# A two-layer decode step on one core: scores of a head first, then the weighted sum of the head ahead

## The chip, the cores and the metric

The kernel runs on one core of one Trainium2 chip. The metric is the device time of one execution in microseconds. Before the change it is 2555.6 us, the median of three runs (2555.37 to 2556.39). A core has five engines that run side by side and synchronise by semaphores: TensorE (matrix products, PE in the profile), VectorE (DVE), ScalarE (ACT), GpSimd (POOL) and SyncE (SP). Sixteen DMA engines move data from HBM into the on-chip memory; here all transfers are issued by SyncE, in one fixed order.

## The reference

Two layers of the same weights. Each layer normalises x (2 batch entries, 576 columns), attends over a cached K and V, adds, then runs a mixer with a gated two-matrix network, and adds again:

```
q = (LN(x) @ wq) as 32 heads of 128
p = softmax(q . K / sqrt(128))          # K: 2 x 32 x 16384 x 128, bf16
x = x + (p @ V) @ wo                    # V like K
y = LN(x); h = gelu(LN(y) @ w1); hs = shift(h) @ w2
x = x + (y + hs) + gelu(LN(y + hs) @ w3) @ w4     # w3: 576 x 4608, w4: 4608 x 576
```

With one token the shifts along the sequence leave only zeros, so hs is the product of zeros with w2. The cache is 64 tiles (2 batch entries x 32 heads) of K and 64 of V, each 16384 x 128 in bf16, 4.19 MB. Both layers read the same cache.

## The kernel before

The memory `mem` holds six slots of one cache tile each, and ahead of them a small area for three buffers of transposed K (`kt`), which also takes weights between the attentions. A tile lies as 128 partitions of 128 rows of 128, so one transfer has 128 pieces of 32 KB. `plan_all` writes out every transfer with its place, in one list. `Store.pump` issues the next entry as soon as the program has given back all the cells under it (`Store.release`); SyncE then waits at that entry for the instructions that read those cells last, and everything behind it waits too. At the end of layer 0 three K tiles and two V tiles stay in memory (`held`), so layer 1 starts with head 63, then 61, 62, 0, 1 and so on (`order`). In this stretch slot 0 takes the weights wo, w3, w4 and layer 1's wq, one into the place of another: w3's first block into the place of the first group of wo, w4's groups into the places of w3's blocks.

A head (`attention`, the loop over s) has 128 blocks of 128 cache rows. Half are scored on TensorE: a chunk of eight blocks is transposed (L1161), copied by ScalarE into `kt` (L1177) and multiplied with q as a column (L1187), with the scores two chunks behind the transposes (`LEAD`). The other half is scored on VectorE in four pieces, a product with q spread over all partitions (L1218) and a sum (L1222), in `dots`. `softmax_max` takes the maximum of both parts (L1228, L1230, L1232) and over the partitions on GpSimd (L1235); `softmax_exp` takes the exponentials on ScalarE (L1243 to L1249); `pv` multiplies V in four pieces of 32 blocks (L1275). `q_broadcast` prepares q of the next head: a column (L1112), a diagonal (L1118), a product with ones (L1122), a copy (L1125). While head s is scored, the PV of head s - 1 is done: chunks 0 to 3 of head s, then each of the chunks 4 to 7 followed by one piece of PV. `landed` (relayed by GpSimd, L187) tells TensorE and VectorE that a tile has come.

The loop runs over heads 1 to 63 as 21 turns of three heads, on TensorE, ScalarE and VectorE (`Graph.loop`, `_loop`). The loop's first instruction is set at slot 0 of an instruction block on each of the three engines. At the end of a turn each engine lowers the semaphores it has used by what one turn adds.

After the loop `last_head` finishes head 63: softmax, `shares` (sums of exponentials, L927), `normed`, `dealt` (the heads' outputs put in the order that wo needs, L950 to L961), PV and five groups of wo (`heads_projection`, L903). `two_norms` then does both layer norms ahead of w3 from one set of sums, `cols_projection` multiplies w3 (L830, L840), `gelu` follows, and `groups_projection` multiplies w4 in eight groups (L903). In layer 0, `ahead` and `lay` use free moments of this stretch to transpose and copy 16 chunks of layer 1's first K tile (14 chunks to be laid, two held over), so that layer 1 can begin with `early_scores` (L1203).

Of the kernel before, what the change touches and what calls it, by code (L numbers as in the profile page):

```python
# [32 lines left out]
class Graph:  # L33
# [72 lines left out]
    def loop(self, first, turns, step):  # L106

        for e, a in first.items():
            n = len(self.ops[e]) - a
            assert n % turns == 0  # L110
            self.loops.append((e, a, n // turns, turns, step))
# [33 lines left out]
    def emit(self):  # L145
# [8 lines left out]
        for e, first, n, turns, _ in self.loops:  # L154
# [38 lines left out]
        def runner(e):  # L193
# [3 lines left out]
            def run(eng):  # L197
                seen, taken = {}, {}
                i = 0
                while i < len(ops):  # L200
                    if i in loops:
                        n, turns, step = loops[i]
                        self._loop(eng, e, i, n, turns, step, taken, seen, sems, wait, needs, emit_op)
                        i += n * turns
                        continue
# [12 lines left out]
    def _loop(self, eng, e, first, n, turns, step, taken, seen, sems, wait, needs, emit_op):  # L218
# [29 lines left out]
        for k, v in per.items():  # L248
            most = max(need.get(k, 0) for need in rel)
            assert most >= v > 0, (e, k, v, most)  # L250
        assert all(v > 0 for need in rel for v in need.values())
        me = eng.engine
        with self.nc.Fori(0, (turns - 1) * step + 1, step, engines=OrderedEngineSet([me]), head_slot={me: 0}) as turn:
# [79 lines left out]
class KB:  # L333
# [14 lines left out]
    PK = ["prod", "gT", "hf", "every"]  # L348
    GROUPS = (6, 6, 6, 6, 6, 3, 2, 1)

# [158 lines left out]
    def plan_all(self):  # L509
# [22 lines left out]
        self.plan_cols("w3", 0, self.w3, [full(0, mt, a), full(1, mt, a + w3r), full(2, mt, a + 2 * w3r),  # L532
                                          full(4, mt, a + 3 * w3r), (3, 0, mt // 2, 0), (3, mt // 2, mt, a)])
# [212 lines left out]
    def two_norms(self, l):  # L746
# [6 lines left out]
        self.scale_of()  # L753
        self.stt(s[:, 4, :], s[:, 2, :], -LN_EPS, hm[:, 1, :], ALU.mult, ALU.add, ["s2", "hm"], ["s4"])
        self.tt(s[:, 5, :], self.mv[:, 0, :], hm[:, 0, :], ALU.mult, ["mv", "hm"], ["s5"])
        self.tt(s[:, 5, :], self.mv[:, 2, :], s[:, 5, :], ALU.subtract, ["mv", "s5"], ["s5"])
        self.stt(s[:, 5, :], s[:, 5, :], 2.0, s[:, 3, :], ALU.mult, ALU.mult, ["s5", "s3"], ["s5"])
        self.tt(s[:, 4, :], s[:, 4, :], s[:, 5, :], ALU.add, ["s4", "s5"], ["s4"])
        self.recip(s[:, 6, :], s[:, 4, :], ["s4"], ["s6"])
# [3 lines left out]
        self.centred(self.x, "x")  # L763
        self.tt(self.kb(self.y0), self.kb(self.xc), self.over_k(s[:, 3, :]), ALU.mult, ["prod", "s3"], ["prod"])
        self.tt(self.kb(self.y), self.kb(self.y0), self.hsc[:, :, :], ALU.add, ["prod", "hsc"], ["prod"])
        self.tt(self.xn[:, :, :], self.kb(self.y), self.over_k(s[:, 7, :]), ALU.mult, ["prod", "s7"], ["xn"])

    def between_norms(self):
# [3 lines left out]
        self.tt(self.x1[:, 0:n, :], y0[:, 0:n, :], self.hs[:, 0:n, :], ALU.add, ["prod", "hs"], ["x1"])  # L772
        self.tt(self.x1[TL:, n, :], y0[TL:, n, :], self.hs[TL:, n, :], ALU.add, ["prod", "hs"], ["x1"])
        self.dv(lambda e: e.tensor_copy(out=self.xb[:, 0:n, :], in_=y0[:, 0:n, :]), reads=["prod"], writes=["xb"])
        self.dv(lambda e: e.tensor_copy(out=self.xb[TL:, n, :], in_=y0[TL:, n, :]), reads=["prod"], writes=["xb"])
# [225 lines left out]
    def attention(self, l):  # L1001
# [5 lines left out]
        def step(s, c, more):  # L1007
            h, u = c // n, o[s]
            if more:
                self.transposes(l, s, u, c)  # L1010
                pend.append((s, u, c, self.chunk))
                self.chunk += 1
                self.evacuate(pend[-1][3])
            while len(pend) > LEAD:
                self.scores(*pend.pop(0))
        if l == 0:
# [6 lines left out]
            for c in range(2 * n):  # L1023
                step(0, c, True)
                if c % n in (0, 2):
                    self.dots(l, 0, o[0], c // n, c % n // 2)
                if c == 2 * n - 2:
                    self.q_broadcast(1)
        else:
# [3 lines left out]
            for h, b, col in sorted(self.early):  # L1033
                self.early_scores(l, o[0], h * self.BP + b, col)
                if (h, b) == (0, self.CH):
                    self.q_broadcast(1)
            self.store.claim("kt", 0, self.AUX)
            for x in pend:
                self.evacuate(x[3])
            w = self.NB - 2 * self.PB  # L1040
            self.dv(lambda e: e.tensor_copy(out=self.s_dve[0][:, 0:w], in_=self.sps[2][:, 2 * self.PB:self.NB]),
                    reads=[("sps", 2)], writes=[("s_dve", 0)], to="vector")
        first = self.g.mark()
        for s in range(1, U):
            u, before = o[s], o[s - 1]
            self.landed("k", u, True)
            for c in range(2 * n):
                step(s, c, True)
                if c % n in (0, 2):
                    self.dots(l, s, u, c // n, c % n // 2)  # L1050
                if c == 2 * n - 2:
                    self.q_broadcast(s + 1)
# [312 lines left out]
```

## Time and profile before

| | |
|---|---|
| median of three runs | 2555.6 us |
| the profiled execution | 2555.16 us |
| its span, first to last instruction | 2553.4 us |
| mean granted TensorE clock | 0.572 |
| busy: PE, DVE, ACT, POOL | 64%, 74%, 48%, 6% |
| read from HBM | 1094.21 MB, 429 GB/s over the span |

How to read it: the page gives each engine's busy time, the span in 40 slices, the DMA queues, the chain of work that ended last, and groups of instructions. In a row by stretch the columns are: from and to, length, busy time and count of PE, PEld (weight loads), DVE, ACT and POOL, then the granted TensorE clock, the share of time in which the DMA engines were busy, and the rate in GB/s. In a timeline row they are: start, duration, engine, line, operation, output and inputs, shape, count, and in brackets the idle time ahead of it with what ended it. In a row of a group they are: busy time and mean ns of one, then idle time with its releaser. In a row of DMA issues the last column is the median time from issue to landing.

### The profile page before, as it was taken

Reading aid. Unit: us, or ns where it says so; the run is one execution under the profiler, and the core shown is the slowest. Engines: PE = TensorE matmul, PEld = TensorE weight load, DVE = VectorE, ACT = ScalarE, POOL = GpSimd, SP = SyncE. Lnnn points to the kernel's source line nnn. Section 1 sums busy time; section 2 is a strip of 40 time slices with the busy share of each in tenths; the row PEclk is TensorE's granted clock in tenths of the full one; section 3 lists DMA queues with packets and bytes.
Section 4 is the critical chain, followed back from the end, with each engine's and each line's share of the span. In section 5 each row is a group of like instructions: output and inputs, shape, how many; then the busy total and the mean of one; then the engine's idle time right before and its main releaser. Section 6 shows DMA issues by size and latency. Waiting matters only on the chain.

```text
span 2553.4 us, 75093 instructions
## 1 busy us (share of the span) xinstructions
PE 1629.1 (64%) x34456; PEld 1592.5 (62%) x34456; DVE 1889.3 (74%) x1924; ACT 1215.6 (48%) x1831; POOL 160.5 (6%) x151
## 2 busy tenths in 40 slices
PE   3766666656666665666687756666665666666566
PEld 3766566656656665666677756656665666666565
DVE  4877777777777777777649877777777777777774
ACT  2544444544444454444456544444454444445442
POOL 0000000000000000000000000000000000000000
PEclk8555655555555555555555565555555555555555
DMA  9999999999999999999999999999999999999999
GB/s 410 429 433 431 432 432 431 432 431 433 431 432 432 432 433 430 434 430 432 424 398 428 431 432 432 431 432 431 433 431 433 431 431 433 432 432 431 432 432 383
DMA packets 44761, 1094.82 MB, mean 429 GB/s; under 512 B 4906, under 2 KB 6318, under 8 KB 9390
## 3 DMA queue, kind: packets, MB, share of 16 engines
q1 hardware_dynamic: 44718, 1094.23, 99.9%
q8 instruction: 29, 0.48, 0.1%
q14 instruction: 14, 0.11, 0.0%
HBM read 1094.21 MB, written 0.00 MB: 429 GB/s over the span
## 4 chain that ended last, share of the span: by engine, by line
DMA 63%; DVE 21%; issue 9%; PE 5%; DVEq 0%; SPq 0%; ACT 0%; POOLq 0%; ACTq 0%
DMA mem<-in_A_k_cache_dram 61%; DVE prod L1218 10%; DVE s_dve L1222 9%; DMA mem<-in_B_w_dram 2%; PE tps L1161 2%; PE mps L1275 2%; PE sps L1122 1%; DMA mem<-in_A_wq_dram 0%; PE sps L1187 0%; DVE diag L1118 0%; PE sps L903 0%; DVE mx L1232 0%; DVE q_col L1112 0%; DVE o_acc L1256 0%; DVE mx L1230 0%
## 5 line engine op out<-in xcount | busy, mean ns | idle before, releaser
L1177 ACT ACTIVATE mem<-tps 128x1024 bf16<-128x1024 bf16 x1018 | 1030.1, 1024 | 848.5 <-PE tps L1161 826.8
L1222 DVE TENSOR_REDUCE s_dve<-prod 128x16 f32<-128x2048 bf16 x508 | 1161.2, 2286 | 17.4
L1161 PE MATMUL tps<-ident,mem 128*128 128x128 bf16 x8256 | 1011.0, 301 | 152.9 <-POOLq L187 148.1
L1218 DVE TENSOR_TENSOR prod<-mem,qb 128x2048 bf16<-128x2048 bf16 x508 | 621.3, 1223 | 534.0 <-POOLq L187 512.2
L1275 PE MATMUL mps<-p,mem 128*128 128x1 bf16 x16384 | 515.5, 166 | 605.7 <-ACT p L1249 605.7
L1275 PEld LDWEIGHTS mps<-p,mem 128*128 128x128 bf16 x16384 | 487.8, 105 | 616.5 <-ACT p L1249 616.4
L1161 PEld LDWEIGHTS tps<-ident,mem 128*128 128x128 bf16 x8256 | 770.0, 136 | 162.5 <-POOLq L187 157.4
L1187 PEld LDWEIGHTS sps<-q_col,mem 128*128 128x128 bf16 x8144 | 410.5, 113 | 5.0 <-ACT mem L1177 4.8
L1187 PE MATMUL sps<-q_col,mem 128*128 128x1 bf16 x8144 | 398.2, 170 | 4.3 <-ACT mem L1177 4.1
L1235 POOL PARTITION_ALL_REDUCE mx<-mx x128 | 158.6, 1239 | 2339.4 <-DVE mx L1232 2339.4
L1243 ACT ACTIVATE mx<-mx 128x1 f32<-128x1 f32 x128 | 25.9, 203 | 338.8 <-POOL mx L1235 338.8
L1122 PE MATMUL sps<-diag,ones_bf 128*128 128x128 bf16 x129 | 37.0, 287 | 114.0 <-DVE diag L1118 113.9
L1122 PEld LDWEIGHTS sps<-diag,ones_bf 128*128 128x128 bf16 x129 | 13.4, 104 | 124.6 <-DVE diag L1118 124.6
L1125 ACT ACTIVATE qb<-sps 128x128 bf16<-128x128 f32 x129 | 35.8, 278 | 61.7 <-PE sps L1122 61.7
L1245 ACT ACTIVATE p<-s_dve,mx 128x64 bf16<-128x64 f32 x128 | 44.5, 348 | 15.4
L1249 ACT ACTIVATE p<-sps,mx 128x64 bf16<-128x64 f32 x128 | 37.6, 293 | 0.0
L1230 DVE TENSOR_REDUCE mx<-sps 128x1 f32<-128x64 f32 x128 | 27.3, 213 | 6.2 <-PE sps L1187 6.2
L1118 DVE TENSOR_SCALAR diag<-ident,q_f 128x128 bf16<-128x128 bf16 x129 | 31.6, 245 | 0.0
L1228 DVE TENSOR_REDUCE mx<-s_dve 128x1 f32<-128x64 f32 x128 | 26.6, 208 | 0.0
L830 PE MATMUL sps<-xn,mem 128*128 128x2 bf16 x544 | 21.5, 174 | 6.7 <-DMA mem<-in_A_wq_dram 4.8
L1256 DVE COPY o_acc<-mps 128x1 f32 (+1 forms) x130 | 19.2, 148 | 8.4 <-PE mps L1275 8.4
L830 PEld LDWEIGHTS sps<-xn,mem 128*128 128x128 bf16 x544 | 20.6, 122 | 7.8 <-DMA mem<-in_A_wq_dram 5.5
(113 smaller groups left out, 229.1 us busy)
## 6 DMA issues: line engine op xcount, KB each, us to landing
mem<-in_A_v_cache_dram SPq DMA_DIRECT2D x125, 4096.0 KB, 47.2
mem<-in_A_k_cache_dram SPq DMA_DIRECT2D x124, 4096.0 KB, 40.9
mem<-in_B_w_dram SPq DMA_DIRECT2D x10, 864.0 KB, 15.3
mem<-in_A_wq_dram SPq DMA_DIRECT2D x8, 1024.0 KB, 12.6
mem<-in_B_w_dram SPq DMA_DIRECT2D x7, 1152.0 KB, 15.4
mem<-in_A_wo_dram SPq DMA_DIRECT2D x6, 1152.0 KB, 35.8
mem<-in_A_v_cache_dram SPq DMA_DIRECT2D x4, 1024.0 KB, 8.8
mem<-in_A_k_cache_dram SPq DMA_DIRECT2D x2, 2048.0 KB, 10.2
```

The lines of the kernel that those rows point to most:

```text
L830: ins = pe.matmul(out[:, m * B:(m + 1) * B], lhsT=buf[:, c:c + 127 * d + 1:d], rhs=self.xn[:, k, :], start=first and m == lo, stop=False, ...
L1122: self.pe(lambda pe: pe.matmul(qps, lhsT=self.ones_bf[:, :], rhs=self.diag[:, :], start=True, stop=True, skip_group_check=True), reads=["o ...
L1125: self.act(lambda e: e.activation(out=self.qb[s % self.NS][:, :], in_=qps, func=ACT.Copy), reads=[("qps", i)], writes=[("qb", s % self.NS) ...
L1161: ins = pe.transpose(self.tps[t][:, j * 128:(j + 1) * 128], buf[:, j * 128:(j + 1) * 128], self.ident[:, :])
L1177: self.act(lambda e: e.activation(out=self.kt[k], in_=self.tps[t][:, :].rearrange("p (i c) -> p i c", i=self.CH), func=ACT.Copy), reads=[( ...
L1187: ins = pe.matmul(self.sps[sp][:, c * self.CH + j:c * self.CH + j + 1], lhsT=self.kt[k][:, j, :], rhs=self.q_col[:, sp:sp + 1], start=True ...
L1218: self.dv(lambda e: e.tensor_tensor(out=prod, in0=buf.rearrange("p (j d) -> p j d", d=128), in1=qbc, op=ALU.mult), reads=[("qb", s % self. ...
L1222: self.dv(lambda e: e.tensor_reduce(out=sd[:, c0:c0 + DB], in_=prod, axis=AX.X, op=ALU.add), reads=["prod"], writes=[("s_dve", s % self.NS ...
L1235: self.pool(lambda e: e.partition_all_reduce(self.mx[:, 3, m:m + 1], self.mx[:, 2, m:m + 1], channels=128, reduce_op=ROP.max), reads=[("mx ...
L1245: self.act(lambda e: e.activation(out=p[:, n:self.NB], in_=self.s_dve[s % self.NS][:, :], func=ACT.Exp, bias=self.mx[:, 4, m:m + 1], scale ...
L1249: self.act(lambda e: e.activation(out=p[:, 0:n], in_=self.sps[i][:, 0:n], func=ACT.Exp, bias=self.mx[:, 4, m:m + 1], scale=self.scale, acc ...
L1275: ins = pe.matmul(self.mps[:, 448:449], lhsT=buf[:, j * 128:(j + 1) * 128], rhs=p[:, col:col + 1], start=(h == 0 and b == 0), stop=(h == 1 ...
```

## The change

In the words of the code:

- In a head, all eight chunks and their scores come first, then the exponentials of the head before, the spread of the next q, the wait for V and the four pieces of PV. The queue of chunks is emptied in every head (`rest`).
- `q_broadcast` is split: column and diagonal (`q_diag`) at the third chunk, product and copy (`q_spread`) after the exponentials. The maximum over VectorE's scores (`first_max`) moves to the end of its own head; the rest of the maximum and the keeping of the output move ahead of VectorE's second piece.
- The loop's head on TensorE moves from slot 0 to slot 200 (layer 0) and 60 (layer 1); ScalarE's and VectorE's loops have no fixed slot. At the end of a turn each engine waits for the full count of a turn before it lowers a semaphore.
- `last_head` does all of PV ahead of wo, and the dealing of the second part after the first group of wo. The `ahead` and `lay` calls are placed anew, more of them ahead of the last PV and fewer in the steps of w4.
- `early_scores` runs in the order in which chunks were made, VectorE's columns first, into the bank `mps`; their copy and maximum come under the rest.
- w3's first block of layer 0 is loaded as two halves.
- `two_norms` has the same operations in another order, with buffers `y0` and `y` tracked by themselves.

The core of the diff:

```
-        full(0, mt, a), full(1, mt, a + w3r), ...
+        (0, 0, mt // 2, a), (0, mt // 2, mt, a + w3r // 2), full(1, mt, a + w3r), ...
-            if i < 5:
+            if i < 3:
                 self.ahead(l, 1)
-            if i < 6:
+            if i < 4:
                 self.lay(l, 1)
...
         for s in range(1, U):
-            u, before = o[s], o[s - 1]
-            self.landed("k", u, True)
+            self.landed("k", o[s], True)
             for c in range(2 * n):
-                step(s, c, True)
-                if c % n in (0, 2):
-                    self.dots(l, s, u, c // n, c % n // 2)
-                if c == 2 * n - 2:
-                    self.q_broadcast(s + 1)
+                step(s, c)
                 if c == LEAD:
                     self.keep_o(s - 2)
                     self.softmax_max(s - 1)
-                if c == n:
-                    self.softmax_exp(s - 1)
-                    self.landed("v", before, False)
-                if c >= n:
-                    self.pv(l, s - 1, before, c - n)
-        self.g.loop(first, (U - 1) // NS, NS)
-        self.ahead(l, 1)
-        while pend:
-            self.scores(*pend.pop(0))
+                if c % n in (0, 2):
+                    self.dots(l, s, o[s], c // n, c % n // 2)
+                if c == LEAD:
+                    self.q_diag(s + 1)
+            self.first_max(s)
+            rest()
+            self.softmax_exp(s - 1)
+            self.q_spread(s + 1)
+            self.landed("v", o[s - 1], False)
+            for g in range(4):
+                self.pv(l, s - 1, o[s - 1], g)
+        self.g.loop(first, (U - 1) // NS, NS, self.HEAD[l])
+        self.ahead(l, 2)
+        self.lay(l, 2)
         self.store.release("kt")
         self.last_head(l, U - 1, o[U - 1])
...
+        self.softmax_max(s)
+        self.keep_o(s - 1)
         self.dv(... every ...)
-        self.softmax_max(s)
-        self.keep_o(s - 1)
         self.shares(0, first)
         self.normed(l, 0, first)
+        self.ahead(l, 1)
         self.dealt(0, late, ...)
+        self.ahead(l, 1)
         self.softmax_exp(s)
         self.touch(ACT.Sqrt)
+        self.lay(l, 2)
+        self.landed("v", u, False)
+        for g in range(4):
+            self.pv(l, s, u, g)
+        self.shares(first, U)
+        self.keep_o(s, None)
+        self.heads_projection(l, 0)
+        self.normed(l, first, U)
+        self.dealt(late, U, ...)
+        self.heads_projection(l, 1)
+        self.ahead(l, 1)
         self.lay(l, 1)
-        self.shares(first, U)
-        self.landed("v", u, False)
-        self.pv(l, s, u, 0)
-        self.heads_projection(l, 0)
-        for g in range(1, 4):
-            self.pv(l, s, u, g)
-        self.keep_o(s, None)
-        self.normed(l, first, U)
-        self.heads_projection(l, 1)
-        self.dealt(late, U, ...)
```

In `_loop`, and in the early part of layer 1:

```
-        with self.nc.Fori(..., head_slot={me: 0}) as turn:
+        with self.nc.Fori(..., head_slot={me: slot} if slot else None) as turn:
...
+            wait(eng, per, inside)
             for k, v in per.items():
                 eng.sem_inc(sems[k], -v)
...
-            for h, b, col in sorted(self.early):
+            for i, (h, b, col) in enumerate(self.early):
                 self.early_scores(l, o[0], h * self.BP + b, col)
-                if (h, b) == (0, self.CH):
+                if i == 1:
                     self.q_broadcast(1)
+                if i == w // self.CH - 1:
+                    self.dv(... s_dve[0] <- mps ...)
+                    self.first_max(0)
```

More of the change, by code (lines that the diff above doesn't have):

```diff
@@ L104, in mark, with loop @@
         return {e: len(self.ops[e]) for e in ("tensor", "scalar", "vector")}
-    def loop(self, first, turns, step):
+    def loop(self, first, turns, step, slot):
         for e, a in first.items():
@@ L216, in emit, with _loop @@
                     sect(runner(e))
-    def _loop(self, eng, e, first, n, turns, step, taken, seen, sems, wait, needs, emit_op):
+    def _loop(self, eng, e, first, n, turns, step, slot, taken, seen, sems, wait, needs, emit_op):
         ops = self.ops[e]
@@ L1005, in attention, with step, rest @@
         pend = []
[L1007 to L1014, printed above, removed]
+        def step(s, c):
+            self.transposes(l, s, o[s], c)
+            pend.append((s, o[s], c, self.chunk))
+            self.chunk += 1
+            self.evacuate(pend[-1][3])
+            if len(pend) > LEAD:
+                self.scores(*pend.pop(0))
+        def rest():
+            while pend:
                 self.scores(*pend.pop(0))
```

83 lines of the change are left out of this document (48 added, 35 removed).

## The prediction

> **What bounds the kernel now.** I read the page first, then busy time by stretch, then SyncE's order of issues, then the timeline of the stretch that loses time.
>
> ```profile
> span 2553.4 us, 75093 instructions
> DMA  9999999999999999999999999999999999999999
> q1 hardware_dynamic: 44718, 1094.23, 99.9%
> q8 instruction: 29, 0.48, 0.1%
> mem<-in_A_v_cache_dram SPq DMA_DIRECT2D x125, 4096.0 KB, 47.2
> mem<-in_A_k_cache_dram SPq DMA_DIRECT2D x124, 4096.0 KB, 40.9
> ```
>
> The DMA engines are busy in every slice. A cache tile lands 41 to 47 us after its issue, while its own bytes take 4.194 MB / 432 GB/s = 9.7 us: some four tiles are queued ahead of it. So only what empties that queue can move the end. The stretches (after PEclk: DMA share, then GB/s) show where it empties:
>
> ```profile
> 30.00:110.00 80.00, 51.84 (x1049) 50.48 (x1049) 71.85 (x69) 42.59 (x63) 4.99 (x4) 0.63 1.00 429
> 200.00:1200.00 1000.00, 627.62 (x13203) 614.87 (x13203) 756.54 (x725) 478.06 (x722) 65.17 (x52) 0.57 1.00 432
> 1262.00:1270.00 8.00, 6.46 (x155) 6.20 (x154) 2.48 (x8) 3.33 (x8) 0.35 (x1) 0.50 1.00 418
> 1270.00:1294.00 24.00, 19.12 (x448) 18.10 (x446) 5.46 (x34) 7.20 (x12) 0.00 (x0) 0.50 0.99 372
> 1294.00:1332.00 38.00, 29.66 (x641) 28.16 (x638) 16.82 (x35) 19.64 (x27) 1.25 (x1) 0.50 1.02 423
> 1332.00:1360.00 28.00, 21.16 (x440) 20.76 (x439) 26.21 (x27) 17.48 (x27) 2.51 (x2) 0.62 0.97 398
> 1420.00:2500.00 1080.00, 684.18 (x14399) 670.33 (x14396) 820.60 (x785) 522.65 (x785) 69.94 (x56) 0.57 1.00 432
> 2508.00:2546.00 38.00, 26.13 (x689) 24.94 (x687) 9.82 (x54) 7.96 (x18) 0.35 (x1) 0.50 1.00 408
> ```
>
> The attention loops run at 432. Weights with a full queue give 418 to 423 (1262:1270, 1294:1332). Two holes stand out: **A**, 1270 to 1294, 24 x (1 - 372/421) = 2.8 us; **B**, 1332 to 1360, 28 x (1 - 398/432) = 2.2 us. The closing weights (2508:2546) have a full queue already; their 408 is their small rows.
>
> Why they empty: each SyncE issue waits until its buffer is given back.
>
> ```profile
> 1269.00 0.33 SPq L98 DMA_DIRECT2D mem<-in_B_w_dram  x1
> 1272.63 0.33 SPq L98 DMA_DIRECT2D mem<-in_B_w_dram  x1
> 1275.95 0.33 SPq L98 DMA_DIRECT2D mem<-in_B_w_dram  x1
> 1282.73 0.33 SPq L98 DMA_DIRECT2D mem<-in_B_w_dram  x1
> 1284.29 0.33 SPq L98 DMA_DIRECT2D mem<-in_B_w_dram  x1
> 1326.26 0.33 SPq L98 DMA_DIRECT2D mem<-in_A_k_cache_dram  x1
> 1335.69 0.33 SPq L98 DMA_DIRECT2D mem<-in_A_k_cache_dram  x1
> 1337.76 0.33 SPq L98 DMA_DIRECT2D mem<-in_A_v_cache_dram  x1
> 1351.28 0.33 SPq L98 DMA_DIRECT2D mem<-in_A_k_cache_dram  x1
> ```
>
> In A, w3's second and third blocks go out at 1272.63 and 1275.95 (after the wo groups in whose place they lie), w3's last half block at 1282.73, and the first w4 groups only at 1284.29. In B the two halves of one K tile are 9.4 us apart, and the next K tile goes out at 1351.28.
>
> **The change part by part.** A, on TensorE: head 63's first chunk, its last scores, its PV, the dealing, wo, then the residual sum, the normed x, w3:
>
> ```profile
> 1243.46 1.04 PE L1161 MATMUL tps<-ident,mem 128*128 128x128 bf16 x8 [1.31 <-POOLq L187]
> 1262.49 0.61 PE L1187 MATMUL sps<-q_col,mem 128*128 128x1 bf16 x16
> 1266.91 0.99 PE L1275 MATMUL mps<-p,mem 128*128 128x1 bf16 x32
> 1268.83 2.70 PE L1275 MATMUL mps<-p,mem 128*128 128x1 bf16 x96
> 1274.48 0.38 PE L950 MATMUL sps<-otn,prod 128*128 128x16 bf16 x8 [1.88 <-issue]
> 1275.78 1.21 PE L903 MATMUL sps<-oB,mem 128*128 128x2 bf16 x40
> 1277.02 0.35 DVE L595 TENSOR_TENSOR st<-st,sps 128x8 f32<-128x8 f32 x2 [1.51 <-PE sps L903]
> 1280.95 0.19 PE L798 MATMUL mps<-xn,prod 128*128 128x2 bf16 x1
> 1281.00 4.81 PE L830 MATMUL sps<-xn,mem 128*128 128x2 bf16 x108
> ```
>
> Today head 63's scores end at 1263.1, because its chunks alternate with head 62's PV; the softmax then gates the last PV, which ends at 1271.5. After the change no chunk waits for V. One head, from its K landing:
>
> ```profile
> L1222 DVE TENSOR_REDUCE s_dve<-prod 128x16 f32<-128x2048 bf16 x4 | 9.1, 2285 | 0.1
> L1177 ACT ACTIVATE mem<-tps 128x1024 bf16<-128x1024 bf16 x8 | 8.2, 1024 | 6.8 <-PE tps L1161 6.7
> L1161 PE MATMUL tps<-ident,mem 128*128 128x128 bf16 x64 | 8.1, 309 | 1.3 <-POOLq L187 1.3
> L1218 DVE TENSOR_TENSOR prod<-mem,qb 128x2048 bf16<-128x2048 bf16 x4 | 4.9, 1224 | 4.6 <-POOLq L187 4.5
> L1275 PE MATMUL mps<-p,mem 128*128 128x1 bf16 x128 | 4.0, 165 | 4.8 <-ACT p L1249 4.8
> L1235 POOL PARTITION_ALL_REDUCE mx<-mx x1 | 1.3, 1254 | 18.2 <-DVE mx L1232 18.2
> ```
>
> TensorE: eight chunks of some 1.07 us (transposes; the scores overlap) = 8.6, the last copy 1.0, exponentials 1.1 (an estimate: four small ScalarE operations), PV 4.0: 14.7 us. VectorE: 4 x (1.22 + 2.29) = 14.0 plus some 1.3 of small ones = 15.3. Both fit in the 19.4 us that two tiles take on the DMA. Head 63's scores now end near 1253 and VectorE's part near 1259; maximum, all-reduce and exponentials (0.6 + 1.3 + 1.1) are done by 1262 to 1263, and V63 lands two tiles after K63: 1243.4 + 19.4 = 1262.8. Ahead of this PV TensorE now does four chunks of layer 1's transposes (4.3 us), the shares and the first dealing; it is free for them from 1257. PV runs about 1263.3 to 1267.3; then shares, wo 0, dealing, wo 1, one chunk, wo 2 to 4: 1.0 + 1.2 + 0.4 + 1.1 + 1.0 + 1.2 + 1.2 = 7.1, so the residual sum comes at 1274.4 and not 1277.02. The 1.88 us that TensorE lost to "issue" may come back at another place: then 1276.3.
>
> - Norms reordered: some 20 small operations in sequence fill the 3.9 us from residual sum to normed x, 0.2 us each; two of them leave the dependent sequence: 0.4 us.
> - w3's first block in two halves: one more issue, 0.33 us on an idle SyncE; half of 36 matmuls earlier (0.8 us) for the last half block.
> - So w3 starts at 1278 (or 1279.8) and has finished its second block at 1281.2 (or 1283). With today's bytes and a full queue, DMA runs dry at about 1285; an issue needs about 2 us to first data, so w4's first groups must go out by 1283. Both values hold. I take hole A as closed: 2.8 gained; worst case with the stall 0.5 less.
> - Transposes moved out of the w4 steps and the copies with them (1.0 us each on TensorE and ScalarE): from behind DMA waits to the wait for V; nothing on the path. If V came before them, 2 us would go to it.
>
> B: K tile 61's second half is given back after chunk 7 and the fourth product. Today chunks 4 to 7 stand behind PV steps: 1335.7. After, with its start 2.6 us earlier, TensorE leaves it 8.6 us after the loop's start, against 14 today: at about 1327.6 where the DMA needs it by 1332. V63 follows by 1333 (needed by 1337), K62 by 1342.5 (needed by 1346.5; VectorE sets it). Each has some 4 us to spare; hole B closes, 2.2 gained.
>
> - Early scores: VectorE's columns first and into another bank, copy and first maximum under the rest: the first product starts up to 1.9 us earlier, inside the same slack; no issue depends on it.
> - q split in two, the spread after the exponentials: the next head's products wait for it, but they wait for K anyway; without that cover about 0.7 us a head.
> - Maxima moved ahead of the second product: 0.2 + 0.2 + 0.2 us of VectorE, moved, not added. SyncE keeps its order; GpSimd's relays stay where they were, the all-reduce between them.
> - Extra waits at the turn's end: the signals have arrived in the turn already; the next turn's first chunk and product stand behind them; 0, at most 0.1 us a turn.
> - Fetch slots: no row shows another slot. The nearest is today's entry of the layer 1 loop, 4.0 us of "issue" ahead of its first chunk; the new one costs between nothing and twice that, taken as the same, and B's slack covers up to 4 more.
>
> ```profile
> 1321.67 1.03 PE L1161 MATMUL tps<-ident,mem 128*128 128x128 bf16 x8 [3.96 <-issue]
> ```
>
> Not all of 2.8 + 2.2 = 5.0 can come back: instruction blocks pass over the same engines. 0.1% of 2553 us over 29 packets is some 0.07 each, and about one every 6 us of new code falls in both stretches, so 8 x 0.07 = 0.5 stays, less the 0.2 that the stretch between the holes can give. **Sum: 4.7 us.** 2553.4 - 4.7 = 2548.7 of span; this execution took 2555.16, 1.8 more than its span, and the median is 0.44 above it: 2550.9.
>
> The Trainium skill (Runtime: NRT & Kernel Launch, section on instruction fetch mechanics) says that a taken branch to a page outside the fetched window stalls until that page has come. The 3.96 us row agrees. By it every turn of the long TensorE loop pays a stall wherever its head lies, and so slots alone would give nothing; the sum above gives them nothing either.
>
> The Trainium skill (Perfetto Trace Analysis, section on DMA optimizations) has two rules that pull apart: larger DMAs use the memory better, and splitting lets some start sooner where engines are idle. The split w3 rows are 4.6 KB against 9.2 KB; by the first rule the split would lose a little. The stretch 1294:1332 with rows of 1 to 8 KB still gives 423 against 418 for 9 KB rows, so the first rule does not show at this size.
>
> **Rivals.**
> - *Only A closes*: the first turn of layer 1 stalls on instruction blocks by more than its 4 us of slack. For it: the 3.96 us at the entry. Gain 2.5: 2553.1.
> - *Only B closes, or nothing*: a fetch stall of 3 us or more falls between V and w3's second block, and w4 goes out at 1284.3 as today. Against: even with today's 1.88 it is in time. Gain 2.0 or none: 2553.6 to 2555.6.
> - *More closes*: the small losses around the holes and in the first 110 us go too (30:110 ran at 429, 0.6 us). Gain 5.2 to 6: 2550.4 to 2549.6.
> - *Slower*: PV no longer fills TensorE's waits, so a head is a serial chain of 14.7 us, and new slots add fetch stalls in every turn. It decides from 19.4 - 14.7 = 4.7 us a head (14 a turn); every 0.1 us beyond costs 126 x 0.1 = 13 us: 2564. Against: one stall of 4 us a turn is under a third of that slack.
>
> **How the numbers follow.** About 0.2% (5.1 us) is what a measurement of this kernel can tell from no change; the forecast lies just inside. Forecast (4.2 to 5.1 gained) 0.50; more 0.27; only A 0.11; only B or nothing 0.06; slower 0.06. Faster by over 0.2% is "more" and the upper edge of the forecast: 0.31; within 0.2%: 0.62; slower: 0.07. The range, 2549.8 to 2553.4, leaves out the far end of "more", half of "only B", and "slower". The likeliest case alone is 2550.5 to 2551.4.
>
> **What would show it.** Right: 1270 to 1294 at some 415 GB/s and no stretch below 428 from 1330 to 1370; residual sum near 1274.4; the w4 issue by 1283; K 61's halves 4 to 5 us apart; attention still at 432; weights at the end as today. Step A is wrong if w4 goes out after 1284, step B if a cache tile is issued under 2 us before the queue runs out, and all of it if the loops fall below 432.

## The result and the profile after

The changed kernel takes 2552.26 us (median of 22 runs, 2552.00 to 2552.90), the kernel before, timed in turn with it, 2555.91 us (22 runs, 2554.41 to 2558.26). The ratio is 0.9985, with a 95% interval of 0.9979 to 0.9992: faster by 0.15%, inside the forecast range and within the 0.2% that was called no change. The profiled execution took 2552.28 us against 2555.16 before, so the two traces have 2.9 us to explain; the prediction gave 4.7. (By the medians it is 3.65 us, as the profiled execution of the kernel before lies 0.75 us under its median.)

From the page of the changed kernel: span, DMA queues, the chain that ended last, and two groups.

```profile
span 2550.6 us, 75213 instructions
q1 hardware_dynamic: 44862, 1094.23, 100.0%
q8 instruction: 28, 0.46, 0.1%
DMA 71%; DVE 19%; issue 8%; PE 1%; SPq 0%; POOLq 0%; DVEq 0%; ACT 0%
L1184 PE MATMUL tps<-ident,mem 128*128 128x128 bf16 x8256 | 823.3, 271 | 707.8 <-POOLq L187 707.2
L1300 PE MATMUL mps<-p,mem 128*128 128x1 bf16 x16384 | 450.7, 165 | 85.3 <-POOLq L187 78.2
```

TensorE's PV now waits for V to land and hardly for ScalarE's exponentials. The stretches of the prediction, in the changed kernel:

```profile
1262.00:1270.00 8.00, 7.20 (x226) 7.23 (x227) 1.02 (x5) 1.59 (x2) 0.00 (x0) 0.50 1.01 417
1270.00:1294.00 24.00, 19.68 (x398) 18.39 (x396) 4.76 (x35) 9.36 (x13) 0.00 (x0) 0.50 1.02 414
1294.00:1332.00 38.00, 30.40 (x701) 28.23 (x698) 18.86 (x35) 18.06 (x28) 1.25 (x1) 0.59 1.02 423
1332.00:1360.00 28.00, 22.15 (x513) 20.94 (x512) 27.55 (x27) 16.91 (x28) 2.51 (x2) 0.75 1.01 419
1420.00:2500.00 1080.00, 635.17 (x14345) 598.94 (x14344) 819.36 (x784) 475.75 (x784) 70.16 (x56) 0.65 1.00 432
2508.00:2546.00 38.00, 23.86 (x639) 22.46 (x637) 6.52 (x44) 5.56 (x11) 0.00 (x0) 0.50 0.97 395
```

Hole A (1270 to 1294) rose from 372 to 414 GB/s and is closed; hole B (1332 to 1360) from 398 to 419, where 428 was forecast; the loop stays at 432. The closing weights seem to fall from 408 to 395, but this row ends at 2546 us, when some DMA engines of the faster kernel have nothing left to load. Between 2512 and 2540 us, where all of them still load, the two kernels (before, then changed) are alike:

```profile
2512.00:2540.00 28.00, 17.93 (x479) 17.27 (x479) 7.54 (x40) 4.88 (x14) 0.00 (x0) 0.50 1.02 413
2512.00:2540.00 28.00, 16.18 (x402) 15.05 (x398) 5.25 (x36) 3.67 (x7) 0.00 (x0) 0.50 1.02 412
```

The granted clock in the loop went from 0.57 to 0.65. From the timeline of the changed kernel: last PV of layer 0, residual sum, w3, a w4 issue, the entry of layer 1's loop, and the issues of the loads that refill K61's buffer in two halves and of the next K tile (k2 in the expectations):

```profile
1262.80 3.55 PE L1300 MATMUL mps<-p,mem 128*128 128x1 bf16 x128 [1.55 <-POOLq L187]
1274.62 0.35 DVE L596 TENSOR_TENSOR st<-st,sps 128x8 f32<-128x8 f32 x2 [5.46 <-PE sps L908]
1278.37 3.25 PE L835 MATMUL sps<-xn,mem 128*128 128x2 bf16 x72
1281.65 0.33 SPq L98 DMA_DIRECT2D mem<-in_B_w_dram  x1
1315.61 2.61 PE L1184 MATMUL tps<-ident,mem 128*128 128x128 bf16 x23
1323.55 0.33 SPq L98 DMA_DIRECT2D mem<-in_A_k_cache_dram  x1
1331.00 0.33 SPq L98 DMA_DIRECT2D mem<-in_A_k_cache_dram  x1
1345.81 0.33 SPq L98 DMA_DIRECT2D mem<-in_A_k_cache_dram  x1
```

The residual sum comes at 1274.62 (forecast 1274.4, before 1277.02), w4 at 1281.65 (by 1283; 1284.29). The loop's entry shows no "issue" any more. But K61's second half goes out at 1331.00, not 1327.6, and the next K tile at 1345.81, not 1342.5.

The stream of loads can be followed more closely: each transfer signals 16 completions, which I read as one from each DMA engine. The last of the 16 is its landing, and the time between the first and the last is called the spread here. These landings (us, from the completions in the two traces) give a ledger of the 2.9 us:

```
                         before    after    gained so far   in this step
K63                      1243.36   1242.07      1.29         +1.29
V63                      1262.80   1262.62      0.18         -1.11
last w4 of layer 0       1301.86   1299.43      2.43         +2.25   (hole A)
V61, last part           1323.40   1321.54      1.86         -0.57
fourth transfer behind
  K61 (a K tile)         1384.56   1380.28      4.28         +2.42   (hole B)
last cache tile          2511.47   2507.40      4.07         -0.21
last w4 of layer 1       2549.88   2547.01      2.87         -1.20
```

The two holes gave 2.25 + 2.42 = 4.67 us, close to the 4.7 of the prediction, though its two holes had 2.8 + 2.2 = 5.0. What it did not have are the other rows: +1.29, and -1.11, -0.57, -0.21 and -1.20. The experiments look for both: which part of the change closed the holes, and where the rest went.

### The profile page after: what moved, and what is told of

Its sections match the earlier page's. It is cut to its first block, busy times and chain, and to the rows that moved or that the text cites. A ratio compares the mean times of both kernels' runs of the same rounds, so it can differ in the third digit from the quotient of the medians.

```text
span 2550.6 us, 75213 instructions
## 1 busy us (share of the span) xinstructions
PE 1522.6 (60%) x34456; PEld 1432.9 (56%) x34456; DVE 1888.3 (74%) x1924; ACT 1113.7 (44%) x1831; POOL 162.1 (6%) x151
## 4 chain that ended last, share of the span: by engine, by line
DMA 71%; DVE 19%; issue 8%; PE 1%; SPq 0%; POOLq 0%; DVEq 0%; ACT 0%
DMA mem<-in_A_k_cache_dram 64%; DVE s_dve L1244 9%; DVE prod L1240 9%; DMA mem<-in_A_wo_dram 3%; DMA mem<-in_B_w_dram 2%; DMA mem<-in_A_v_cache_dram 2%; DMA mem<-in_A_wq_dram 0%; DVE mx L1249 0%; PE tps L1184 0%; DVE diag L1138 0%; DVE mx L1257 0%; SPq L98 0%; DVE q_col L1129 0%; DVE o_acc L1281 0%; DVE mx L1255 0%
## 5 line engine op out<-in xcount | busy, mean ns | idle before, releaser
L1200 ACT ACTIVATE mem<-tps 128x1024 bf16<-128x1024 bf16 x1018 | 955.7, 1036 | 1290.0 <-PE tps L1184 1287.5
L1184 PE MATMUL tps<-ident,mem 128*128 128x128 bf16 x8256 | 823.3, 271 | 707.8 <-POOLq L187 707.2
L1184 PEld LDWEIGHTS tps<-ident,mem 128*128 128x128 bf16 x8256 | 677.6, 124 | 717.7 <-POOLq L187 716.8
L1300 PE MATMUL mps<-p,mem 128*128 128x1 bf16 x16384 | 450.7, 165 | 85.3 <-POOLq L187 78.2
L1300 PEld LDWEIGHTS mps<-p,mem 128*128 128x128 bf16 x16384 | 443.3, 103 | 100.2 <-ACT p L1274 97.0
L1210 PE MATMUL sps<-q_col,mem 128*128 128x1 bf16 x8144 | 368.7, 167 | 159.2 <-ACT mem L1200 142.9
L1210 PEld LDWEIGHTS sps<-q_col,mem 128*128 128x128 bf16 x8144 | 320.3, 101 | 217.4 <-ACT mem L1200 212.7
L1145 PE MATMUL sps<-diag,ones_bf 128*128 128x128 bf16 x129 | 29.8, 231 | 21.6 <-DVE diag L1138 21.6
L1274 ACT ACTIVATION_READ_ACCUMULATOR p<-sps,mx (+1 forms) x128 | 24.2, 189 | 0.0
```

The source lines that it names most:

```text
L1145: self.pe(lambda pe: pe.matmul(qps, lhsT=self.ones_bf[:, :], rhs=self.diag[:, :], start=True, stop=True, skip_group_check=True), reads=["o ...
L1184: ins = pe.transpose(self.tps[t][:, j * 128:(j + 1) * 128], buf[:, j * 128:(j + 1) * 128], self.ident[:, :])
L1200: self.act(lambda e: e.activation(out=self.kt[k], in_=self.tps[t][:, :].rearrange("p (i c) -> p i c", i=self.CH), func=ACT.Copy), reads=[( ...
L1210: ins = pe.matmul(self.sps[sp][:, c * self.CH + j:c * self.CH + j + 1], lhsT=self.kt[k][:, j, :], rhs=self.q_col[:, sp:sp + 1], start=True ...
L1274: self.act(lambda e: e.activation(out=p[:, 0:n], in_=self.sps[i][:, 0:n], func=ACT.Exp, bias=self.mx[:, 4, m:m + 1], scale=self.scale, acc ...
L1300: ins = pe.matmul(self.mps[:, 448:449], lhsT=buf[:, j * 128:(j + 1) * 128], rhs=p[:, col:col + 1], start=(h == 0 and b == 0), stop=(h == 1 ...
```

## Experiments

All were timed beside the kernel before, whose median was 2555.98 to 2556.22 there. In the expectations, "the last transfer" and "the end at 2546.5" are the landing one before the last; in the kernels that they speak of, the last w4 lands some 0.36 us later.

**Which part closed the holes.** First, the order within a head alone:

```
-    HEAD = (200, 60)                  +    HEAD = (0, 0)
-    (0, 0, mt // 2, a), (0, mt // 2, mt, ...)   +    full(0, mt, a), ...
     last_head, groups_projection, two_norms as before
```

> The order within a head alone: the changed kernel with the fetch slots, the whole w3 block, the last head and the norms of before. Theory (the order within a head closes the first hole by itself, and the slots are worth the 0.6 us that the run at slot 0 showed): residual sum at 1274.8, w4's first block issued at about 1282, a wait of 4 us at the entry of layer 1's loop, time 2552.9 within 0.4. Rival (the parts need one another): sum at 1276.3 or later, w4 at 1283.5 or later, time near 2554.5.

It took 2553.70 us (2552.87 to 2555.19), 0.4 us above the theory's range. All the rest of the change without it (`step`, `dots`, `pv`, `q_broadcast` and `early_scores` as before; slots, w3, last head and norms as after):

> All of the change but the order within a head: the kernel before with the fetch slots 200 and 60, the split w3 block, the new last head and the reordered norms; scores and PV of a head are still mixed, q and the maxima stand where they did. Theory: the residual sum stays near 1277, w4 near 1284, K61's second half and k2 go back no sooner than in the kernel before less what the entry of the loop no longer waits, time 2555.3 within 0.5. Rival (the last head's order and the slots carry half of the gain): sum at 1275.5, time near 2553.8.

It took 2557.68 us (2556.86 to 2559.04), ratio 1.0005 (0.9996 to 1.0014): not to be told from the kernel before, and 2.4 us above what was expected. Two timeline rows of the first kernel, then two of the second, and its row for the stretch of hole A:

```profile
1274.68 0.36 DVE L596 TENSOR_TENSOR st<-st,sps 128x8 f32<-128x8 f32 x2 [3.52 <-PE sps L904]
1281.94 0.33 SPq L98 DMA_DIRECT2D mem<-in_B_w_dram  x1
```

```profile
1277.13 0.16 DVE L596 TENSOR_TENSOR st<-st,sps 128x8 f32<-128x8 f32 x1 [4.48 <-PE sps L908]
1329.36 1.01 PE L1284 MATMUL mps<-p,mem 128*128 128x1 bf16 x32 [5.64 <-ACT p L1258]
```

```profile
1270.00:1294.00 24.00, 20.57 (x449) 19.62 (x449) 5.11 (x35) 8.27 (x13) 0.00 (x0) 0.57 0.96 376
```

The order within a head closes hole A by itself (sum at 1274.68); without it the sum stays at 1277.13 and the stretch at 376 GB/s. Most of hole B hangs on it too: from V61's last part to the fourth transfer behind K61 the last completions lie 61.17 us apart in the kernel before, 59.73 with the order alone, 58.74 in the changed kernel, and 62.36 without the order. The kernel without it is spared the stall at the loop's entry and loses it again five chunks later: TensorE stands 5.64 us before the first piece of PV, with chunks 5 to 7 behind it, and K61's second half goes out at 1336.40. The clock granted over the run was 0.652 with the new order and 0.574 without.

Then the last head's order, put back alone:

```
-        self.ahead(l, 2); self.lay(l, 2)     +        self.ahead(l, 1)
-        last_head(): PV, then wo             +        last_head(): PV 0, wo 0, PV 1 to 3, wo 1 ...
-            if i < 3: ahead / i < 4: lay     +            if i < 5: ahead / i < 6: lay
```

> The changed kernel with the last head of each layer in the order of before (its PV in pieces between the first wo rows, the transposes for layer 1 after w4's groups 0 to 4). Theory (the last head's own order closes the first hole): the residual sum is back at 1276.5 to 1277.0 instead of 1274.6, w4 is issued at about 1284 instead of 1281.65, the time lost between 1262 and 1302 rises from 0.58 us to about 2.5, and the kernel ends 1.9 us later, near 2554.2. Rival (the order within a head closes it, since the exponentials stand earlier): sum at 1274.6, time 2552.3 within 0.3.

It took 2552.27 us (2552.03 to 2552.59), with the sum at 1274.77. The rival holds: the last head's order, taken alone, is worth nothing. Next the two parts that the prediction put at nothing:

```
-    (0, 0, mt // 2, a), (0, mt // 2, mt, ...)   +    full(0, mt, a), ...
     two_norms, between_norms as before
```

> The changed kernel with the whole first w3 block and the norms in the order of before: the two parts that the prediction put at nothing, since w3 waits for its weights by then. Theory: xn 0.5 us later, w3's first matmuls at 1278.8 to 1279, the waits for w3's later blocks shorter by the same, w4 issued within 0.4 of 1281.65, time 2552.3 within 0.3. Rival (they carry what the run with the order within a head alone lacked beside the slots, 0.8 us): w4 at 1282.3 or later, time 2553.0.

It took 2552.12 us (2551.83 to 2552.64), with w4 issued at 1281.70: these parts are worth nothing, as forecast. Then the slots:

```
-    HEAD = (200, 60)
+    HEAD = (0, 0)          # head_slot on all three engines
```

> The changed kernel with the loops at the fetch slots of before (0 on every engine). Theory (the slots take away the stall of TensorE at the entry of layer 1's loop and that is worth part of the second hole): a wait of some 4 us on TensorE after 1315 is back, K61's halves go back near 1327 and 1333, k2 near 1347, and the kernel ends 1.0 to 1.3 us later, 2553.3 to 2553.6. Rival, that of the prediction (the slots are worth nothing, since VectorE's dots give the halves back): issues at 1323.6, 1331.0 and 1345.8 as in the changed kernel, time 2552.3 within 0.4.

It took 2552.88 us (2552.56 to 2553.52), 0.6 more than the changed kernel. From its timeline, the entry of layer 1's loop and the issue of K61's second half:

```profile
1320.83 2.74 PE L1184 MATMUL tps<-ident,mem 128*128 128x128 bf16 x24 [4.01 <-issue]
1332.60 0.33 SPq L98 DMA_DIRECT2D mem<-in_A_k_cache_dram  x1
```

The stall of 4 us is back and the issue 1.6 us later. So the slots are worth something, though half of what I had expected here. That the stall is what costs the 0.6 us is not shown: in the stretch of hole B the last engine needs 59.12 us against 58.74, only 0.38 more, and the rest lies in steps where instruction fetches fall (below). The kernel with the new order alone also has slot 0 (its entry shows 4.43 us). It needs 0.8 us more than the kernel at slot 0, though the parts in which the two differ cost nothing singly. Its runs scatter by 2.3 us, and its profiled execution ended its loads at 2547.51, sooner than the 2547.90 of the kernel at slot 0. This stays open.

**What holds K61's second half.** In the code SyncE waits, for a product that signals VectorE itself, on the next VectorE instruction that signals the other engines (`_stand_in`). In the changed kernel that is `first_max`, behind the 2.29 us sum. From its timeline on VectorE, the last product and sum of K61 and that maximum:

```profile
1327.13 1.22 DVE L1240 TENSOR_TENSOR prod<-mem,qb 128x2048 bf16<-128x2048 bf16 x1
1328.39 2.29 DVE L1244 TENSOR_REDUCE s_dve<-prod 128x16 f32<-128x2048 bf16 x1
1330.71 0.22 DVE L1249 TENSOR_REDUCE mx<-s_dve 128x1 f32<-128x64 f32 x1
```

The experiment puts a tiny copy between product and sum for it to wait on:

```
         self.used(l, "k", u, b0, DB)
+        if i == 1:
+            self.dv(lambda e: e.tensor_copy(out=self.tick[:, :], in_=self.eps[:, :]), reads=["eps"], writes=["tick"])
         self.dv(... tensor_reduce(out=sd[:, c0:c0 + DB], in_=prod ...
```

> The changed kernel, with one tiny VectorE copy (128x1) put between the product and the sum of a K half's second dot step, so that the DMA which refills that half waits for this copy and no longer for what VectorE does after its 2.29 us sum. Theory (what is left of the hole at 1332-1350 hangs on VectorE's sum and first maximum): the second half of K61's buffer is issued at about 1328.6 instead of 1331.00 and k2 at about 1343.3 instead of 1345.81; the time lost between 1332 and 1370 falls from 1.23 us to about 0.4; the kernel ends 0.8 us sooner, near 2551.4. Rival (TensorE's last chunk or SyncE's queue releases that DMA): the issues stay at 1331.0 and 1345.8 and the time at 2552.3. Against both: the copies cost VectorE 0.06 us each, beside a stream that does not wait for it.

The copy and the two issues in its timeline, then two of its stretches:

```profile
1328.14 0.15 DVE L1246 COPY tick<-eps 128x1 f32<-128x1 f32 x1
1328.36 0.33 SPq L98 DMA_DIRECT2D mem<-in_A_k_cache_dram  x1
1343.17 0.33 SPq L98 DMA_DIRECT2D mem<-in_A_k_cache_dram  x1
```

```profile
1332.00:1360.00 28.00, 23.48 (x517) 22.47 (x515) 27.72 (x30) 17.31 (x30) 2.51 (x2) 0.62 1.01 430
2508.00:2546.00 38.00, 23.59 (x630) 22.21 (x627) 6.54 (x44) 5.56 (x11) 0.00 (x0) 0.50 0.95 385
```

The mechanism holds to 0.3 us: the issues come 2.64 us sooner, and the stretch runs at 430. The time does not follow: 2552.32 us (2551.95 to 2552.68). The second row is lower than the 395 GB/s of the changed kernel for the reason given above: the first engine has its last w4 at 2541.14, 2 us sooner, and waits out the rest of the row. Over the stretch of hole B (V61's last part to the fourth transfer behind K61) the last engine needed 58.71 us, in the changed kernel 58.74. So only engines that were ahead had stood still in what was left of the hole. The same kernel once more, for how well this repeats:

> The kernel with the early give-back once more, for how well landings repeat. Theory (fetches fall on the same engines in each execution): landings within 0.2 us of the first profile all along, spread at the end 5.7. Rival (which engine a fetch meets is drawn anew): spreads in the middle and at the end other than 4.1 and 5.7.

It took 2552.22 us (2551.89 to 2552.42). From 30 to 2525 us the landings agree within 0.3 us; between 2530 and 2541 they differ by 0.4 to 0.5, and the last by 0.04. The spreads of the last cache tile and the last w4 are 3.82 and 5.36 us against 4.29 and 5.74. Most of it repeats, not all.

**Fetches.** A fetch is the load of one 16 KB block of instructions (queue q8 on the page) by one DMA engine. Matmuls on unused data add such blocks: the changed kernel's trace has 28 of them, with 128 matmuls 29, with 256 matmuls 30. They were meant to move each later fetch to another engine: one block in layer 0's waits for wq (without and with the early give-back), two blocks, one behind layer 1's loop, and two with one.

```
+    def spare(self, n):      # n matmuls of ident with zeros into a column that is written anew before it is read
...
+            if w == "wq" and l == 0: self.spare([24, 32, 32, 0, 40][i])     # one block
...
+            rest(); self.spare(96); self.q_spread(1)        # two blocks: [28, 36, 36, 0, 60], and this
...
+        if l: self.spare(80)      # behind layer 1's loop: in last_head, before the first dealing,
+        if l: self.spare(48)      # and before its PV
```

> The changed kernel with 128 matmuls on unused data (256 TensorE instructions, one block of 16 KB) put into TensorE's waits for wq in layer 0: one instruction fetch more, and each later fetch is one further in the row. They write a PSUM column that nothing reads before it is written again. Theory (each fetch holds one of 16 DMA engines for 1.05 us, and counts only where it meets the engine that is last): the landing of V63 comes 9.7 us after V62's instead of 10.84, or the step of 10.8 shows at another tile; the spread of the last transfers' 16 completions differs from 3.9 us; the time moves by 0, or by about 1.1 either way, so 2551.2 or 2553.4 are as likely as 2552.3. Rival (a fetch costs its mean, 0.07 us, wherever it falls): landings as in the changed kernel but for 0.07, time 2552.3 within 0.2.

> The early give-back and the 128 matmuls on unused data together. Theory (the end is set by the DMA engine that is last; with the early give-back the 16 engines lost 0.75 us less in the mean, yet the last one ended where it did, with a spread of 5.74 us at the end instead of 3.93; other fetches on other engines give another spread): the spread at the end differs from 5.7 by 1 us or more, and the end moves with it, to between 2550.3 and 2552.3. Rival (the spread does not come of the fetches): spread 5.5 to 6, time 2552.3 within 0.2.

> The early give-back and 256 matmuls on unused data (two blocks more; 160 of them in TensorE's waits for wq, 96 in its wait for q's diagonal in head 0): each later fetch is two further in the row. Theory: again another spread at the end than 5.7, time between 2550.3 and 2552.5, and not the time of the run with one block more except by chance. Rival: spread 5.5 to 6, time 2552.3 within 0.2.

> The early give-back, and one block of 128 matmuls on unused data behind layer 1's loop (80 in TensorE's wait before the last head's shares are dealt, 48 before its PV), so that the fetches of the tail go over other engines and all before 2500 us stays. Theory: up to the second last cache tile (2497.3) all lands as in the run with the early give-back, within 0.2; from the last tile (2507.0) to the last transfer an engine that no fetch meets needs 38.0 us, as the first of the 16 did in all kernels so far, so the end lies between 2545.0 (no fetch meets the late engines: time 2550.9) and 2546.6 or 2547.8 (one or two do: 2552.3 or 2553.5), and not at 2546.5 but by chance. Rival (something else than the fetches holds the end at 2546.5 to 2546.8 where six kernels had it): 2546.5 to 2546.8 again, time 2552.3.

> The same block behind layer 1's loop, in the kernel with the early give-back and two blocks more at the start. There the last cache tile landed at 2508.88 and the last transfer 37.95 us later, so no fetch of the tail met the last engine. Theory: the tile at 2508.9 again within 0.3, the end at 2546.8 or, where a fetch now meets the last engine, up to 2548.2. Rival (something holds the end): 2546.5 to 2546.8.

The times are 2552.35, 2552.43, 2552.45, 2552.45 and 2552.44 us: no run was faster, and the time alone gives the theory nothing. The landings are mixed. With one block V63 comes 10.10 us after V62, and the spread at the end is 3.27 and not 3.93. With the early give-back it is 5.21 with one block (neither side had this) and 3.84 with two, as the theory had it. One block behind the loop changes nothing at the end: the last engine needs 39.86 us for the closing weights, without the block 39.85 (its cache tiles land 0.26 us later in the mean, though nothing ahead of the block was changed). With two and one behind, the last tile is where it was expected, and the landing before the last comes at 2547.08, inside the theory's range. The landings (first and last of the 16 completions, us):

```
                            K63              last cache tile     last w4
                            first    last    first    last       first    last
changed kernel              1239.96  1242.07 2504.68  2507.40    2543.08  2547.01
one block                   1240.24  1243.13 2505.24  2507.72    2543.59  2546.87
early give-back             1240.09  1242.10 2502.75  2507.04    2541.14  2546.89
 with one block             1240.18  1243.54 2503.41  2507.50    2541.87  2547.06
 with two blocks            1240.04  1243.83 2504.98  2508.88    2543.35  2547.19
 with one behind the loop   1240.41  1242.19 2503.07  2507.39    2541.50  2547.24
 with two, and one behind   1240.07  1243.89 2505.00  2508.79    2543.33  2547.43
slot 0                      1240.13  1243.71 2506.58  2509.49    2544.89  2547.90
kernel before               1240.17  1243.36 2508.95  2511.47    2547.32  2549.88
```

The first engine has K63 at 1240.0 to 1240.4 in all of them, while the last has it anywhere from 1242.07 to 1243.89. This goes with the number of blocks fetched before: over all fourteen profiles K63's spread is 1.8 to 2.3 us where eight blocks were fetched before it (the changed kernel and all others with the new slots and no added matmuls there), 2.8 to 3.6 where nine were (the kernel before, both kernels at slot 0, one block added), and 3.8 where ten were.

From the last cache tile on the first engine always needs 38.3 to 38.5 us, the last one between 38.3 and 39.9. Up to 1.5 us lie between the two, the size of one fetch. In the kernel with the early give-back each of these fetches throws one engine back by some 1.5 us (lag is how long after the first engine it completes a transfer, us):

```
fetch at   lag before -> after      eight fetches on   lag before -> after
1288.9     0.82 -> 2.37             1345.2             2.37 -> 3.82
1296.6     0.86 -> 2.34             1351.3             2.38 -> 3.92
1303.8     0.72 -> 2.31             1359.7             2.31 -> 3.84
1311.8     0.99 -> 2.51             2512.5             2.57 -> 4.04
1325.8     2.53 -> 4.05             2527.9             4.24 -> 5.95
1332.0     2.51 -> 4.06             2540.1             4.23 -> 5.76
```

The trace does not number the engines; that fetch n and fetch n + 8 meet the same one is read from the lags, which fit in each pair. With the block behind the loop the pairs fit in the same way (0.77 -> 2.37, then 2.35 -> 3.87; 0.55 -> 2.11, then 1.99 -> 3.44; 2.25 -> 3.79, then 3.74 -> 5.29). So the blocks seem to go over eight of the sixteen engines in turn, and in the kernel with the early give-back alone eight engines end 3.8 us or more behind the first, the other eight within 2.5. From 1259 us on the changed kernel fetches 20 blocks, two or three for each of the eight. Adding one or two at the start only changes when a given engine gets its share, which would explain why the landing of K63 moves by up to 1.8 us and the last one by 0.6. That this share is what holds the end at 2546.9 to 2547.4 in all kernels that have both the new order and the new slots is argued, not shown: a kernel with fewer blocks of TensorE code between the loops was not tried. No version was measurably faster than the changed kernel.

## Why the prediction was right, and where it was not

- **Hole A**: forecast 2.8, landings 2.25 (3.06 by the first engine of each transfer). Rate, residual sum, w4's issue and the mechanism (no chunk waits for V any more) came as worked out; the last head's order, which the working also counted on, was not needed (2552.27 us without it). For the wait from issue to first data the prediction took about 2 us; the trace of before has 1.5 (w4's first group, issued at 1284.29, first packet at 1285.77).
- **Hole B**: forecast 2.2, landings 2.42. The steps inside were wrong: K61's second half was to leave with TensorE at 1327.6, with 4 us to spare. With an earlier give-back the half went out at 1328.36, so TensorE was done by then (in the changed kernel its PV behind K61's chunks starts at 1325.09); the give-back hung on VectorE's sum and first maximum, 1331.00. The rate of the stretch showed that (419, not 428). It cost next to nothing (58.71 against 58.74 us for the last engine), since what stood still then were engines that were ahead.
- **The sum**: 5.0 less 0.5 plus 0.2. The failed step is the term "some 0.07 each, ... so 8 x 0.07 = 0.5 stays". It divided the fetches' time by the sixteen engines. By the lags a fetch costs its engine some 1.5 us, and the landings move by 1.5, nothing or something between, by how far that engine is from being last. What stands in its place is the rest of the ledger: -1.11 at V63 (the fetch at 1259.4; in the kernel before none fell there), -0.57 by 1321 (the one at 1317.9), -0.21, -1.20 in the closing weights (38.41 to 39.61 us for the last engine, 38.37 to 38.40 for the first), and +1.29 up to K63, where the first engines differ by 0.2: nine blocks are fetched before it in the kernel before, eight in the changed one. Slot 0 alone brings the ninth block back, with K63 at 1243.71; the kernel with the slots and the old order has eight, with K63 at 1242.15. So this row comes of the slots. All rows together give -1.8, where the prediction took off 0.3 net. 4.67 - 1.80 = 2.87 is what the two profiles show. That the -0.21 is a fetch is not shown.
- **Weights at the end as today**: right for the rate (413 and 412 GB/s, the first engine 38.37 and 38.40 us) and wrong for the last engine, by 1.20 us: the fetches at 2518.5, 2527.9 and 2537.9 met engines close to the last one, whose lag was 2.7 (lags 2.2 -> 3.6, 2.2 -> 3.8, 2.4 -> 4.0). The prediction put the 408 down to small rows. In that kernel's trace the stretch lacks its share between 2508 and 2512 (357 GB/s), while the last cache tile lands; the smallest rows, at its end, run at 415 (2540 to 2546).
- **Slots at nothing, covered by B's slack**: wrong by 0.6 us. The stall at the entry is there at slot 0 (4.01 us) and gone at slot 60, but the stretch of hole B accounts for only 0.38 us of the loss, and slot 0 also brings one block more before K63. The Trainium skill (Runtime: NRT & Kernel Launch, section on instruction fetch mechanics) has a taken branch to a page outside the fetched window stall until that page has come, from which the prediction took a stall in every turn. The traces do not bear that out for this loop: neither the kernel before nor the changed one fetches a block between 1371 and 2512 us, where all but the first of layer 1's 21 turns lie. The 3.96 us row stands at the loop's entry, before any turn has ended.
- **Norms, split w3 block, place of the moved transposes, at nothing**: right, 2552.12 and 2552.27 us without them. The row 1294:1332, which the prediction read as rows of 1 to 8 KB, also holds 32 KB rows from 1320.5 us on, so the run without the split is the better evidence.
- **The range**: 2552.26 lies inside it, but 1.4 us above the forecast of 2550.9, outside the likeliest case (2550.5 to 2551.4) and short of "only A closes" (2553.1). That it lies inside is in part luck: +1.29 up to K63, which no term of the sum had, offsets the fetch at V63 (-1.11).
- **Slower**: the loop kept 432 GB/s; a head's serial chain had room enough.

## What to carry to other kernels

Where a kernel is bound by its DMA engines, work with the landing of the last of the sixteen completions and not with GB/s: a hole that only engines with a lead feel costs nothing, and closing it gains nothing. A rate over a row that ends after the first engines have finished reads too low. Straight code has a price there too, since each block of it that is fetched takes some 1.5 us from one data engine in these traces. And when a buffer's give-back is to come sooner, look up which instruction the waiting DMA really waits for; here it was not the one that read the buffer last, and one copy of 0.15 us moved it by 2.64 us.

## What the runs showed of the hardware

- The completions of one transfer spread over 1.8 to 5.8 us, and the spread lasts for 1,000 us: in the changed kernel it was 2.50 us at 1370 and 2.73 at 2507. In the traces of before and after it shrank where the queue ran dry (3.20 us to 1.89 in hole A before, 3.94 to 2.50 in hole B after).
- Each 16 KB block of instructions goes over one DMA engine, its packet takes some 1.05 us, and the engine falls some 1.5 us behind; that eight engines take turns is inferred from the lags above.
- The slot of a loop's head decides whether a block more is fetched: at slot 0 nine blocks came before K63, at slot 200 eight, and K63 landed 1.6 us later at slot 0 (1243.71 against 1242.07).
- 128 matmuls on unused data in a wait of TensorE moved the landing of K63, 1,200 us later, by 1.1 us, its first engine by only 0.3.
- The granted clock in the loop is 0.65 with scores first and PV behind them, and 0.57 with the two mixed; it moved no landing in the loop, which stayed at 432 GB/s.
